# Gate logits with both halves of the gate weights side by side in one 40-column product

## The chip, the core and the metric

The kernel runs on one core of a Trainium2 chip. The engines named below are TensorE (PE; its weight loads are listed apart as PEld), VectorE (DVE), ScalarE (ACT), GpSimd (POOL) and SyncE (SP, which issues most DMAs). The metric is the device time of one execution in microseconds (us), the median of the runs. "The profile" is one execution taken by the hardware profiler.

## The reference, cut to what matters

Clustered attention over 4 batches of 8 heads with 768 positions of 64 numbers, and on its output a mixture of experts with two levels of gates: a group out of four, an expert out of four in that group.

```python
mask = q_assign[:, :, :, None] == k_assign[:, :, None, :]
scores = np.where(mask, scale * np.matmul(q, k.transpose(0, 1, 3, 2)), -1e9)
x = softmax(scores) @ v                      # (3072, 512) after the heads are joined
g_logits = x @ w_group                       # 4 columns
e_logits = xg @ w_expert[g]                  # 4 columns for each of 4 groups
h = np.maximum(xg[mask_e] @ w1[g, e], 0.0)   # 512 -> 1024
out[tok_idx] = combined[:, None] * (h @ w2[g, e])
```

The 4 + 16 gate columns stand in one weight matrix of 20 columns. Its product with x is what is called the logits here.

## The kernel before

**Precision.** Every large product is made of float16 halves: a number is held as a high part and a low part (the rest after rounding), and three products are summed in float32: high with high, high with low, low with high. The product of two low parts is left out.

**Stages.** The attention (function `attention`) goes through 32 heads with 9 units each. For a unit the code issues fine scores (`fine`, L342 and L343 on PE, the exponential L347 on ACT, the low part of the probabilities L349 on POOL), a coarse unit some way ahead (`coarse`, L302 on PE, a row maximum L305 on DVE), the product with V of a unit five units back (`av`, L368 and L369 on PE), and then one or two jobs out of a table of due times (`beside`): loads, splits, cluster assignments, and the gate's work. From about 421 us on the experts follow: a first expert with its rows of the first three batches (`part_a`, L950 and L968), and while it runs the gate's decision for the last batch, then the ranked experts (`ranks`).

**The gate.** Two heads fill 128 columns of x, so the logits of a batch are summed over four steps k, one after each second head. `Router.logits` does a step in two groups of three row tiles (i = 0, 1): six transposes (L592), one copy to SBUF (ACT, L595, tile xTr), nine products of 20 columns (PE, L600: three row tiles, three products each), and an addition to the running sum lg (DVE, a copy L604 at k = 0, an addition L606 later). There are 4 x 4 x 2 = 32 such groups. After k = 3 `Router.decide` takes the largest logit in every group of four and the softmax weights (DVE, L624 to L646, the exponential L635 on ACT), counts the rows of every expert with 12 products (PE, L651, L653, L655), works out the slot of every row (DVE, L658 to L663), and sends six scatters from POOL's queue to a table in DRAM (L674).

**What sets the order.** The sequence of the calls is written out by hand through due times; within a short horizon the framework's scheduler orders the instructions of an engine by a model of their times, so a changed duration can move its neighbours. Instructions of one engine run in that order, and an instruction that waits holds up all behind it on its engine.

**After the last decision.** When the last batch's rows have landed in the table, SP loads it to SBUF (tile tb, L1084), PE sorts it into slots (L1114), the gathers of the first ranked expert follow from it. On PE, 48 products of the first expert's second layer (L968) stand ahead of L1114, and 24 directly behind.

Of the kernel before, what the change touches and what calls it, by code (L numbers as in the profile page):

```python
# [11 lines left out]
F16 = mybir.dt.float16  # L12
BF16 = mybir.dt.bfloat16
F32 = mybir.dt.float32
I32 = mybir.dt.int32
AF = mybir.ActivationFunctionType
ALU = mybir.AluOpType
# [5 lines left out]
P = 128  # L23
# [4 lines left out]
WRS = 16.0  # L28
# [496 lines left out]
class Router:  # L525
# [9 lines left out]
    def setup(self):  # L535
        nc, const, N, E, BS, KD = self.nc, self.const, self.N, self.E, self.BS, self.KD
        wf = const.tile([P, KD, 20], F32, name="wf")
        nc.sync.dma_start(out=wf, in_=self.wr)
        self.WR = const.tile([P, 2, KD, 20], F16, name="WR")
        nc.vector.tensor_scalar(out=self.WR[:, 0], in0=wf, scalar1=WRS, scalar2=None, op0=ALU.mult)  # L540
        nc.vector.scalar_tensor_tensor(out=self.WR[:, 1], in0=wf, scalar=WRS, in1=self.WR[:, 0], op0=ALU.mult, op1=ALU.subtract)
        self.ones = const.tile([P, P], F16, name="ones")
        nc.vector.memset(self.ones, 1.0)
        self.low = const.tile([P, P], F16, name="low")
        nc.gpsimd.affine_select(out=self.low, in_=self.ones, pattern=[[1, P]], compare_op=ALU.is_gt, fill=0.0, base=0, channel_multiplier=-1)
        self.desc = const.tile([P, 30, 4], F16, name="desc4")
        nc.gpsimd.iota(self.desc, [[0, 30], [-1, 4]], base=4, channel_multiplier=0, allow_small_or_imprecise_dtypes=True)
        self.ebase = const.tile([P, E], F32, name="ebase")
        nc.gpsimd.iota(self.ebase, [[BS, E]], base=0, channel_multiplier=0, allow_small_or_imprecise_dtypes=True)
        self.cb = const.tile([P, E], F32, name="cb")  # L550
        NT = N // P
        self.pay = const.tile([P, NT, 2], F32, name="pay")
        nc.gpsimd.iota(self.pay[:, :, 0], [[P, NT]], base=0, channel_multiplier=1, allow_small_or_imprecise_dtypes=True)
        zrow = const.tile([P, 2 * KD], F16, name="zrow")
        nc.vector.memset(zrow, 0.0)
        nc.sync.dma_start(out=self.xbuf[N:N + 1].rearrange("o (p x) -> (o p) x", p=P), in_=zrow)
        em = self.em = const.tile([P, (E + 1) * BS // P // 5, 2], F32, name="em")
        nc.vector.memset(em[:, :, 0:1], float(N))
        nc.vector.memset(em[:, :, 1:2], 0.0)
        self.lg, self.last, self.sent, self.apart, self.done = {}, {}, [], True, -1  # L560

        self.reset()
# [8 lines left out]
    def store(self, b, xs):  # L571

        T = xs.shape[1]
        t0 = b * T
# [4 lines left out]
    def logits(self, b, xs, k, banks=None):  # L579

        nc = self.nc
        T = xs.shape[1]
        n = T // 2
        if k == 0:
            self.lg[b] = self.sm.tile([P, T, 20], F32, name="lg", bufs=2)
        for i in range(2):
            yield PSM, 0, 1
            pool, nm = (banks or [(self.psm, "psm")] * 2)[i]
# [5 lines left out]
            xT = self.sm.tile([P, n, 2, P], F16, name="xTr", bufs=2)  # L594
            self.last["a"] = nc.scalar.copy(out=xT, in_=tp)  # L595
            yield PSM, 1, 1
            lp = pool.tile([P, 512], F32, name=nm)[:, 0:n * 20].rearrange("p (c x) -> p c x", x=20)
            for c in range(n):
                for j, (a, w) in enumerate(((0, 0), (0, 1), (1, 0))):
                    nc.tensor.matmul(out=lp[:, c], lhsT=xT[:, c, a], rhs=self.WR[:, w, k], start=j == 0, stop=j == 2)  # L600
            yield
            lg = self.lg[b][:, n * i:n * i + n]
            if k == 0:
# [11 lines left out]

    def decide(self, b, early=None, then=None):
        nc, sm, E = self.nc, self.sm, self.E
        lg = self.lg[b]
        T = lg.shape[1]
        t0 = b * T  # L620
        G = T * 5
        lv = lg.rearrange("p t (g x) -> p (t g) x", x=4)
# [802 lines left out]
```

## Time and profile before

| | before |
|---|---|
| median of 3 runs | 783.28 us (782.55 to 783.51) |
| profiled execution: time | 782.34 us |
| profiled execution: span from first to last instruction | 780.6 us |
| mean granted TensorE clock | 0.978 of full speed |
| PE busy | 733.3 us (94%), 11086 products |
| PE weight loads busy | 626.5 us (80%) |
| DVE busy | 612.0 us (78%) |
| ACT busy | 466.8 us (60%) |
| POOL busy | 495.6 us (63%) |

The chain that ended last is of no use here: it holds the last four pieces alone, POOL's last scatter of 0.78 us among them. What limits a stretch is read from the busy times by stretch and from who waited for whom. PE runs its products pipelined: the duration of one (171 ns for 20 columns) is its way through the array, and what it costs the engine is the distance between two starts. In the timeline, equal instructions in a row are merged into one line with a count (x9), whose time runs from the first start to the last end; the distance between starts is then read from the start of the next line.

### The profile page before, as it was taken

What the parts mean: (1) busy time and instruction counts of PE and PEld (TensorE: products, weight loads), DVE (VectorE), ACT (ScalarE), POOL (GpSimd) and SP (SyncE); (2) the same over time, 40 slices, a digit from 0 to 9 for tenths busy, and PEclk for the clock granted to TensorE, in tenths of its full rate; (3) what the DMA queues carried; (4) which work ended last, traced back from release to release, by engine and by line L of the source; (5) the groups of instructions that cost most, each with busy time, mean ns of one, the idle gap of its engine ahead of it and who ended that gap; (6) DMA issues with size and microseconds to landing.
All of it is one profiled execution on the core that took longest, in us unless ns stands there. A gap on an engine that the chain in (4) does not pass through costs nothing. (4 is left out here: it accounts for less than half of the span.)

```text
span 780.6 us, 26678 instructions
## 1 busy us (share of the span) xinstructions
PE 733.3 (94%) x11086; PEld 626.5 (80%) x11086; DVE 612.0 (78%) x1209; ACT 466.8 (60%) x910; POOL 495.6 (63%) x497
## 2 busy tenths in 40 slices
PE   5899999999999999998999799999999999999991
PEld 3677888878888788886878677887789999999991
DVE  5998879899798988988875465867789888888830
ACT  5567877768777687775895255444344444555530
POOL 9578787778977788776972445434564655565330
PEclk7899999999999999999999999999999999999996
DMA  8856534435344352223312397866688688889600
GB/s 244 204 144 168 148 102 119 137 94 148 104 119 134 94 149 68 55 94 127 92 30 84 85 313 239 272 224 217 209 265 257 218 259 277 285 255 300 194 32 17
DMA packets 80392, 128.28 MB, mean 164 GB/s; under 512 B 8851, under 2 KB 47251, under 8 KB 80264
## 3 DMA queue, kind: packets, MB, share of 16 engines
q1 hardware_dynamic: 74492, 113.12, 48.9%
q0 software_dynamic: 5616, 13.35, 4.9%
q8 instruction: 88, 1.44, 0.8%
q14 instruction: 40, 0.33, 0.1%
q10 hardware_dynamic: 156, 0.03, 0.0%
HBM read 93.20 MB, written 14.11 MB: 137 GB/s over the span
## 5 line engine op out<-in xcount | busy, mean ns | idle before, releaser
L349 POOL TENSOR_TENSOR pl<-p 128x512 f16<-128x512 f32 x278 | 287.3, 1052 | 84.9 <-ACT p L347 80.7
L305 DVE TENSOR_REDUCE mpart<-psc 128x1 f32<-128x512 f32 (+1 forms) x282 | 189.8, 682 | 35.0 <-PE psc L302 32.8
L347 ACT ACTIVATE p<-psf 128x512 f32<-128x512 f32 x288 | 168.7, 595 | 56.1 <-PE psf L343 49.1
L368 PE MATMUL pso<-V,p 128*128 128x65 f16 x1152 | 161.6, 193 | 0.0
L368 PE MATMUL pso<-V,pl 128*128 128x65 f16 x1152 | 161.2, 194 | 0.0
L369 PE MATMUL pso<-V,pl 128*128 128x64 f16 x1152 | 161.0, 191 | 0.0
L369 PE MATMUL pso<-V,p 128*128 128x64 f16 x1152 | 160.8, 191 | 0.0
L342 PE MATMUL psf<-A 82*128 82x384 f16 (+2 forms) x576 | 143.7, 275 | 4.2 <-ACT p L347 2.8
L343 PE MATMUL psf<-B 128*128 128x384 f16 (+2 forms) x576 | 143.7, 274 | 0.0
L369 PEld LDWEIGHTS <-p 128*128 128x128 bf16 x1152 | 112.6, 98 | 21.4 <-issue 0.2
L368 PEld LDWEIGHTS <-p 128*128 128x128 bf16 x1152 | 112.2, 97 | 9.3 <-issue 1.4
L369 PEld LDWEIGHTS <-pl 128*128 128x128 f16 x1152 | 112.8, 98 | 0.7 <-issue 0.4
L302 PE MATMUL psc<-A 80*128 80x512 f16 (+1 forms) x376 | 108.4, 330 | 5.1 <-DVE mpart L305 3.3
L368 PEld LDWEIGHTS <-pl 128*128 128x128 f16 x1152 | 111.2, 97 | 0.3
L953 DVE SCALAR_TENSOR_TENSOR hl<-psh,hh 128x160 f16<-128x160 f32 (+14 forms) x136 | 49.9, 370 | 58.6 <-ACT hh L952 50.4
L952 ACT ACTIVATE hh<-psh 128x160 f16<-128x160 f32 (+14 forms) x136 | 46.6, 347 | 65.7 <-PE psh L950 64.3
L950 PE MATMUL psh<-xT,wh0a 128*128 128x288 f16 (+7 forms) x512 | 74.7, 255 | 0.0
L1011 POOL DMA_INDIRECT out_dram<-y,ri x32 | 38.5, 1203 | 55.1 <-ACT y L1010 48.8
L912 POOL DMA_INDIRECT xg<-xbuf,ri x32 | 43.5, 1359 | 39.8 <-PE psm L922 25.7
L343 PEld LDWEIGHTS <-B 128*128 128x128 f16 x576 | 56.6, 98 | 13.7 <-issue 5.3
L950 PE MATMUL psh<-xT,wh0b 128*128 128x272 f16 (+6 forms) x448 | 65.2, 254 | 0.9 <-ACT xT L924 0.5
L342 PEld LDWEIGHTS <-A 82*128 82x128 f16 x576 | 55.5, 98 | 12.0 <-DMA A<-mr 0.7
(308 smaller groups left out, 1776.9 us busy)
## 6 DMA issues: line engine op xcount, KB each, us to landing
st<-w SPq DMA_DIRECT2D x128, 512.0 KB
B<-parts SPq DMA_DIRECT2D x64, 192.0 KB
kx<-kT SPq DMA_DIRECT2D x16, 384.0 KB
qx<-qT SPq DMA_DIRECT2D x16, 384.0 KB
vx<-vr SPq DMA_DIRECT2D x16, 384.0 KB
A<-parts SPq DMA_DIRECT2D x32, 192.0 KB
xbuf<-xs SPq DMA_DIRECT2D x4, 1536.0 KB
A<-mk SPq DMA_DIRECT2D x56, 24.0 KB
```

Source lines behind the costliest of these rows:

```text
L302: last["mm"] = nc.tensor.matmul(out=pc[:, off:off + k1 - k0], lhsT=QA[h % 8][0:80, c * P:(c + 1) * P], rhs=KA[h % 8][0:80, k0:k1], start=T ...
L305: nc.vector.tensor_reduce(out=(mp[:, 0, 0:1], mp[:, :, 1], mp[:, 1, 0:1])[i], in_=pc.rearrange("p (a x) -> p a x", a=n), axis=AX.X, op=ALU ...
L342: nc.tensor.matmul(out=o, lhsT=KA[h % 8][0:82, ks], rhs=QA[h % 8][0:82, q0:q1], start=True, stop=False)
L343: nc.tensor.matmul(out=o, lhsT=KBs[h][:, ks], rhs=QBs[h][:, q0:q1], start=False, stop=True)
L347: cfg["exp"] = nc.scalar.activation(out=p32, in_=pf, func=AF.Exp, scale=QK / (SQ * SQ))
L349: lo = (nc.vector if u in (EARLY if h < 2 else DVE_LO[h % 8] if h < NH - 2 else DVE_END) else nc.gpsimd).tensor_tensor(out=pl, in0=p32, in ...
L368: nc.tensor.matmul(out=O[:, col:col + 65], lhsT=p[:, bs], rhs=vh, start=c == 0 and q == 0 and i == 0, stop=False, skip_group_check=True)
L369: nc.tensor.matmul(out=O[:, col:col + 64], lhsT=p[:, bs], rhs=vl, start=False, stop=c == NCH - 1 and i == 1, skip_group_check=True)
L912: self.got = nc.gpsimd.indirect_dma_start(out=xg[0:n].rearrange("p a d -> p (a d)"), out_offset=None, in_offset=bass.IndirectOffsetOnAxis( ...
L950: self.mm = nc.tensor.matmul(out=ph[:, 0:M], lhsT=w[:, k, fs], rhs=xT[:, a, k], start=i == 0, stop=i == 3 * KD - 1)
L952: nc.scalar.activation(out=hh[:, f], in_=ph[:, 0:M], func=AF.Relu)
L953: self.ev = nc.vector.scalar_tensor_tensor(out=hl[:, f], in0=ph[:, 0:M], scalar=0.0, in1=hh[:, f], op0=ALU.max, op1=ALU.subtract)
```

## The change

The gate weights WR are stored as [row, k, part, column] instead of [row, part, k, column], so the 20 columns of the high part and the 20 of the low part lie side by side. For a row tile two products of 40 columns (high and low part of x against both parts of the weights) take the place of three products of 20, so the product of the two low parts is now in it as well. The running sum lg holds 40 columns for a row tile, and `decide` begins with an addition of the two halves into a new tile lgs.

```diff
-        self.WR = const.tile([P, 2, KD, 20], F16, name="WR")
+        self.WR = const.tile([P, KD, 2, 20], F16, name="WR")
...
-            self.lg[b] = self.sm.tile([P, T, 20], F32, name="lg", bufs=2)
+            self.lg[b] = self.sm.tile([P, T, 2, 20], F32, name="lg", bufs=2)
...
-            lp = pool.tile([P, 512], F32, name=nm)[:, 0:n * 20].rearrange("p (c x) -> p c x", x=20)
+            lp = pool.tile([P, 512], F32, name=nm)[:, 0:n * 40].rearrange("p (c w x) -> p c w x", w=2, x=20)
             for c in range(n):
-                for j, (a, w) in enumerate(((0, 0), (0, 1), (1, 0))):
-                    nc.tensor.matmul(out=lp[:, c], lhsT=xT[:, c, a], rhs=self.WR[:, w, k], start=j == 0, stop=j == 2)
+                for a in range(2):
+                    nc.tensor.matmul(out=lp[:, c].rearrange("p w x -> p (w x)"), lhsT=xT[:, c, a], rhs=self.WR[:, k].rearrange("p w x -> p (w x)"), start=a == 0, stop=a == 1)
...
-        lg = self.lg[b]
-        T = lg.shape[1]
+        both = self.lg[b]
+        T = both.shape[1]
+        lg = sm.tile([P, T, 20], F32, name="lgs")
+        nc.vector.tensor_tensor(out=lg, in0=both[:, :, 0], in1=both[:, :, 1], op=ALU.add)
```

Lines behind the addition (L621) are two higher in the changed file: L624 of before is L626 there.

The scheduler places the decision's instructions differently. DVE at the decision of the first batch, before; mpart is the coarse scores' row maximum, rmx to roe are the decision's tiles:

```order
L606 TENSOR_TENSOR lg<-psm,lg 128x60
L624 TENSOR_REDUCE rmx<-lg 128x30
L626 TENSOR_TENSOR req<-lg,rmx 128x120
L305 TENSOR_REDUCE mpart_198<-psc 128x2
L627 TENSOR_TENSOR req<-req,desc_499 128x120
L634 TENSOR_TENSOR rdf<-lg,rmx 128x120
L629 TENSOR_REDUCE rmw<-req 128x30
L631 TENSOR_TENSOR roh<-req,rmw 128x120
L305 TENSOR_REDUCE mpart_198<-psc 128x1
L637 TENSOR_REDUCE rse<-rdf 128x30
L639 TENSOR_TENSOR roe<-roh 128x96
```

DVE at the same place in the changed kernel:

```order
L606 TENSOR_TENSOR lg<-psm,lg 128x120
L621 TENSOR_TENSOR lgs<-lg 128x120
L626 TENSOR_REDUCE rmx<-lgs 128x30
L305 TENSOR_REDUCE mpart_198<-psc 128x2
L628 TENSOR_TENSOR req<-lgs,rmx 128x120
L636 TENSOR_TENSOR rdf<-lgs,rmx 128x120
L629 TENSOR_TENSOR req<-req,desc_499 128x120
L305 TENSOR_REDUCE mpart_198<-psc 128x1
L631 TENSOR_REDUCE rmw<-req 128x30
L639 TENSOR_REDUCE rse<-rdf 128x30
L633 TENSOR_TENSOR roh<-req,rmw 128x120
L641 TENSOR_TENSOR roe<-roh 128x96
```

The addition L621 has come in, and both row maxima still stand between the last logits and roe, each one or two places earlier in the decision. The decisions of the second and third batch read alike.

DVE in the second half of the last batch's decision, before; hl (L953) are evictions of the first expert's hidden layer:

```order
L643 TENSOR_REDUCE res<-rss 128x6
L644 TENSOR_SCALAR res<-res 128x6
L953 SCALAR_TENSOR_TENSOR hl<-psh,hh 128x288
L645 SCALAR_TENSOR_TENSOR res<-rse,res 128x6
L658 TENSOR_TENSOR rps<-psm,cb 128x96
L646 RECIPROCAL pay<-res 128x6
L659 TENSOR_TENSOR rps<-rps,roe 128x96
L664 TENSOR_TENSOR cb<-psm,cb 128x16
L661 TENSOR_REDUCE rds<-rps 128x6
```

DVE at the same place in the changed kernel:

```order
L645 TENSOR_REDUCE res<-rss 128x6
L955 SCALAR_TENSOR_TENSOR hl<-psh,hh 128x288
L646 TENSOR_SCALAR res<-res 128x6
L660 TENSOR_TENSOR rps<-psm,cb 128x96
L647 SCALAR_TENSOR_TENSOR res<-rse,res 128x6
L955 SCALAR_TENSOR_TENSOR hl<-psh,hh 128x288
L648 RECIPROCAL pay<-res 128x6
L661 TENSOR_TENSOR rps<-rps,roe 128x96
L666 TENSOR_TENSOR cb<-psm,cb 128x16
L663 TENSOR_REDUCE rds<-rps 128x6
```

A second eviction of the hidden layer now stands between the counts and the slots. On PE, the products of the first expert are reordered with it: before, 12 of L968 stood between the sixth and the seventh of the eight chunks of L950; now the seventh chunk follows the sixth directly and 7 of L968 stand ahead of the eighth. The 48 products of L968 ahead of L1114 are the same in number.

## Rows read from the trace of the kernel before

**Rows 1.** Busy by stretch: length, PE, PEld, DVE, ACT, POOL busy (instructions), PEclk, DMA share, GB/s

```profile
120.00:150.00 30.00, 29.85 (x586) 24.93 (x584) 26.09 (x59) 23.94 (x46) 22.35 (x22) 1.00 0.44 134
360.00:390.00 30.00, 27.57 (x501) 22.42 (x500) 23.79 (x46) 22.77 (x44) 26.10 (x26) 1.00 0.45 139
```

**Rows 2.** Waits of PE, whole span: us in total, times, longest us

```profile
PE psm L651 <- DVE roe L639: 3.8, 3, 1.3
```

**Rows 3.** Groups by line: count | busy us, mean ns | idle before

```profile
L600 PE MATMUL psm<-WR,xTr 128*128 128x20 f16 x279 | 11.6, 171 | 0.0
L606 DVE TENSOR_TENSOR lg<-psm,lg 128x60 f32<-128x60 f32 x23 | 4.9, 215 | 1.6 <-PE psm L600 1.5
```

**Rows 4.** Timeline of PE, first logits: start us, us, instruction

```profile
94.18 0.19 PE L369 MATMUL pso<-V,pl 128*128 128x64 f16 x1
94.21 0.37 PE L600 MATMUL psm<-WR,xTr 128*128 128x20 f16 x9
94.44 0.22 PE L342 MATMUL psf<-A 82*128 82x128 f16 x1
```

**Rows 5.** Timeline of PE, counts of the last decision; L653 has 80 to 16 columns

```profile
428.80 0.28 PE L653 MATMUL psm<-roe,ones 128*128 128x80 f16 x5
428.94 0.29 PE L655 MATMUL psm<-roe,ones 128*128 128x16 f16 x6
429.09 0.28 PE L950 MATMUL psh<-xTA,wh 128*128 128x288 f16 x1
```

**Rows 6.** Timeline of DVE, decision of the first batch

```profile
153.34 0.22 DVE L606 TENSOR_TENSOR lg<-psm,lg 128x60 f32<-128x60 f32 x1
153.59 0.28 DVE L624 TENSOR_REDUCE rmx<-lg 128x30 f32<-128x120 f32 x1
153.91 0.85 DVE L626 TENSOR_TENSOR req<-lg,rmx 128x120 f16<-128x120 f32 x1
154.68 0.68 DVE L305 TENSOR_REDUCE mpart<-psc 128x2 f32<-128x512 f32 x1
155.28 0.45 DVE L627 TENSOR_TENSOR req<-req,desc 128x120 f16<-128x120 f16 x1
...
156.15 0.82 DVE L631 TENSOR_TENSOR roh<-req,rmw 128x120 f16<-128x120 f16 x1
...
157.67 0.57 DVE L639 TENSOR_TENSOR roe<-roh 128x96 f16<-128x96 f16 x1
```

**Rows 7.** Timeline of POOL, same stretch

```profile
152.58 4.25 POOL L349 TENSOR_TENSOR pl<-p 128x512 f16<-128x512 f32 x4 [1.02 <-ACT p L347]
157.09 1.04 POOL L349 TENSOR_TENSOR pl<-p 128x512 f16<-128x512 f32 x1 [0.26 <-ACT p L347]
```

**Rows 8.** Timeline of PE, same stretch

```profile
158.29 0.20 PE L651 MATMUL psm<-roe,low 128*128 128x96 f16 x1 [1.27 <-DVE roe L639]
```

**Rows 9.** One line's instructions in all four decisions: min/median/max ns

```profile
L626 DVE TENSOR_TENSOR req<-lg,rmx x4: 284/849/849, 153.9 to 427.1; 128x120 f16<-128x120 f32 x4
```

**Rows 10.** Timeline of DVE, decision of the last batch

```profile
429.13 0.45 DVE L953 SCALAR_TENSOR_TENSOR hl<-psh,hh 128x288 f16<-128x288 f32 x1
429.50 0.15 DVE L645 SCALAR_TENSOR_TENSOR res<-rse,res 128x6 f32<-128x6 f32 x1
```

**Rows 11.** Timeline of PE, first expert up to the slots

```profile
438.51 0.41 PE L968 MATMUL psy<-hh,wh 128*128 128x288 f16 x2 [0.99 <-ACT hh L952]
440.01 0.28 PE L968 MATMUL psy<-hh,wh 128*128 128x288 f16 x1 [1.09 <-ACT hh L952]
...
445.98 1.58 PE L1114 MATMUL psm<-perm,tb 16*128 16x16 f32 x12 [1.65 <-DMA tb<-table]
447.50 1.15 PE L968 MATMUL psy<-hh,wh 128*128 128x288 f16 x8
448.49 2.00 PE L968 MATMUL psy<-hh,wl 128*128 128x288 f16 x8
```

**Rows 12.** Busy by stretch, one of the rows at half clock

```profile
450.00:451.00 1.00, 1.00 (x6) 0.60 (x4) 0.56 (x1) 0.00 (x0) 0.69 (x2) 0.50 1.03 395
```

More of the change, by code (lines that the diff above doesn't have):

```diff
@@ L538, in setup @@
         nc.sync.dma_start(out=wf, in_=self.wr)
-        self.WR = const.tile([P, 2, KD, 20], F16, name="WR")
-        nc.vector.tensor_scalar(out=self.WR[:, 0], in0=wf, scalar1=WRS, scalar2=None, op0=ALU.mult)
-        nc.vector.scalar_tensor_tensor(out=self.WR[:, 1], in0=wf, scalar=WRS, in1=self.WR[:, 0], op0=ALU.mult, op1=ALU.subtract)
+        self.WR = const.tile([P, KD, 2, 20], F16, name="WR")
+        nc.vector.tensor_scalar(out=self.WR[:, :, 0], in0=wf, scalar1=WRS, scalar2=None, op0=ALU.mult)
+        nc.vector.scalar_tensor_tensor(out=self.WR[:, :, 1], in0=wf, scalar=WRS, in1=self.WR[:, :, 0], op0=ALU.mult, op1=ALU.subtract)
         self.ones = const.tile([P, P], F16, name="ones")
```

## The prediction

> **What bounds the kernel now.** I read the busy times by stretch first. From 90 us, where the gate's first logits are, to 421 us the attention runs at PE's pace: PE is busy 29.85 of 30 us in a plain stretch, while DVE, the next engine, has 26.1 [rows 1]. So a product less on PE is worth its distance between starts. PE's list of waits then shows the one thing of the gate that holds it: L651, the first count of a decision, waits for the tile roe of DVE, three times and 3.8 us in all [rows 2], 1.27 of it at the first [rows 8]. PE stands behind that product, so a longer decision on DVE is paid in full. Later in that part PE has other idle time too (27.57 of 30 [rows 1]). After 421 us a different chain rules: last logits, decision, scatters, the table's load, and the slots L1114, for which PE waits 1.65 us [rows 11]. Behind L1114 PE is busy again to the end, so what moves L1114 moves the end.
>
> **The products.** Nine products of 20 columns take 0.23 us from the first start to the next instruction, 25.6 ns each [rows 4]. A group has six now. No row shows 40 columns. From below, six products of 16 columns take 0.15 us, 25 ns each; five of 80 to 16 columns, 48 on the mean, take 0.14 us, 28 ns each [rows 5]; 64 columns take 30 ns [rows 4]. So 40 columns cost 25 to 30 ns. I take 26, since the nearest row above, 48 on the mean, has two products of 64 and 80 in it, which pull it up. A group then takes 0.156 us and saves 0.074 (bounds 0.05 and 0.08). Of the 32 groups, 24 lie in the first three batches and 6 of the last batch ahead of the end of the attention: 24 x 0.074 = 1.78 and 6 x 0.074 = 0.44, in sum **-2.2 us** (bounds -1.5 and -2.4). The last two groups lie in the chain to L1114 and are counted there. [...]
>
> **The wider additions.** L606 and L604 go from 60 to 120 elements. L606 has 215 ns [rows 3]; a DVE instruction over 120 elements with nothing in its way has 284 [rows 9]. That is 0.07 more, 32 times, 2.2 us on DVE. It lies beside PE's work, with 4 to 6 us of DVE free in 30 [rows 1]; if that cover were gone it would cost up to the 2.2. Only the last of each batch heads a chain that PE waits for. The strided writes of WR happen once in the setup and I cost them at nothing, beside the attention's first loads.
>
> **The decisions of the first three batches.** L621 is a new link between the last logits and roe, where PE stands. Its size is that of L626, which reads lg from SBUF too: 0.28 us alone and 0.85 in these three decisions [rows 9]. The difference is POOL: L626 begins at 153.91 in the middle of a POOL subtraction and ends at 154.76; four of them run back to back from 152.58 to 156.83, 1.06 us each, so the second ends about 154.7 [rows 6, 7]. L627, L631 and L639 end about 0.1 us behind a POOL instruction in the same way, while the reduction L624 keeps its 0.28. [...]
>
> I walk the new order against these POOL times. L606 now ends at 153.62 and L621 starts at 153.65, just inside the second POOL subtraction, and ends where L626 ended, at 154.76. The reduction L624 takes it to 155.06, the row maximum (0.68) to 155.66. The comparison L626 ends at about 155.8, as L627 did at 155.73. The next two with two SBUF inputs meet the fourth subtraction and end about 157.0. Row maximum and two reductions take it to 158.1 (0.68, 0.28, 0.28, each starting a little before the last ends). L631 then waits out the fifth subtraction, which ends at 158.13, and ends at 158.37; L639 alone takes 0.28 and ends at 158.66. Before, it ended at 158.24. So the chain grows by **0.42 us**, though L621 alone seems to cost 0.85 or 1.1, because other waits for POOL fall away. The low bound is -0.5: of the waits in the rows (L626 0.57, L627 0.17, L631 0.54, L639 0.29 over 0.28) a luckier phase could drop two, about 0.9, against 0.39 for the new link alone (0.07 + 0.32, the step from L624 to L626). The high bound is +1.1, the 0.07 and one POOL subtraction of 1.04 more. Three times: **+1.3 us** (bounds -1.5 and +3.3). Behind L651 wait all of PE's products, and the exponentials that need them.
>
> **The last decision.** POOL is quiet there, so L621 costs its 0.32, the wide L606 0.07, the shorter group of products gives 0.07 back. The order puts a second eviction L953 between the counts and the slots, one step of 0.37 (429.13 to 429.50 [rows 10]). So the scatters start 0.32 + 0.07 - 0.07 + 0.37 = **0.69 us** later (bounds 0.3, if that eviction finds a gap, and 0.75), and table, load and L1114 with them. PE's earlier seventh chunk gains nothing, because PE waits 1.65 us at L1114 anyway [rows 11]; it only gathers PE's idle time there. On SP the register loads for the experts' numbers come a little later among the weight loads, on ACT a few exponentials pass a copy; PE is full there, so I give them nothing.
>
> **Sum.** -2.2 + 1.3 + 0.69 = -0.2 us. The profiled execution took 782.34 us, so the changed one should take 782.1. The median of the runs lies 0.94 above the profiled execution, so **783.0 us** is the forecast. About 0.2% (1.6 us) is what a measurement of this kernel can tell from no change: below 781.7 counts as faster, above 784.9 as slower. The forecast's own range, by a few tenths on each of the three decisions, is 782.0 to 784.5.
>
> **Rivals.** (1) *The products' gain comes through.* If the phase against POOL turns lucky, the three decisions grow by nothing, and the second eviction finds a gap: -2.2 + 0 + 0.3 = -1.9, giving 781.4; with each product at 25 ns 781.2. For it: before, 1.6 us of a decision of 4.9 us are waits for POOL, so there is something to lose. Against it: all three decisions have the same phase, and the walk shows three waits. (2) *The new addition collides with POOL, slower.* If L621 waits for a whole subtraction and no later wait falls away, a decision grows by 1.1: -2.2 + 3.3 + 0.69 = +1.8, giving 785.1. It decides from a growth of 0.5 a decision on ((2.2 - 0.69) / 3), only a tenth above my value; to be seen as slower it takes 1.0. [...] (4) *Wide products cost twice the narrow ones.* At 51 ns a group takes 0.31, and 30 groups lose 2.4 us where the sum has a gain of 2.2: 787.6. The 30 ns of 64 columns speak against it.
>
> **Chances and range.** Forecast 0.57, rival 1 0.19, rival 2 0.12, rival 3 0.10, rival 4 0.02. Faster by over 0.2%: most of rival 1 and a little of the forecast, 0.19. Slower: most of rival 2, half of rival 3, rival 4 and a little of the forecast, 0.20. Within: 0.61. The range goes from rival 1 to rival 2, 781.1 to 785.2, which leaves out about 2 in 10.
>
> **What would show it.** In the profile after: 192 products L600 in groups of six that take about 0.156 us from the first start to the next instruction; L606 at about 0.28; L621 near 0.3 at the last decision and around 1 us at the others; PE's wait at L651 near 1.7 us each instead of 1.27; distance from one decision to the next shorter by 8 x 0.074 - 0.42, about 0.2 us; L1114 at about 445.8; PE's wait ahead of it longer than 1.65. It is wrong if PE's wait at L651 stays at 1.3 or goes over 2.2, if a group of six takes more than 0.18, or if the stretch at 0.50 after L1114 is much longer or gone.

## The result and the profile of the kernel after

The kernel after takes **793.64 us** (median of four runs, 791.12 to 796.41) where the kernel before took 782.91 in the runs beside it: the ratio is put at 1.0124 with a 95% interval of 1.0095 to 1.0153. It is slower, by 10.7 us between the medians; 783.0 was forecast, with a range to 785.2. The profiled execution took 796.41 us with a span of 794.6, the longest of the four; before it was 782.34 and 780.6, so the two profiles lie 14.0 us apart. The mean granted clock was 0.959 in that execution of the kernel after, and 0.978, as in the profile of before, in the one of 791.12, so the clock is not the whole loss. L641, L653, L778 and L1116 of the kernel after are L639, L651, L776 and L1114 of before.

The products did what they should. Group of lines L600 and L606 (count, busy us, mean ns, idle before; [rows 3] answer), and the start of a group of six on PE's timeline:

```profile
L600 PE MATMUL psm<-WR,xTr 128*128 128x40 f16 x186 | 9.6, 181 | 0.0
L606 DVE TENSOR_TENSOR lg<-psm,lg 128x120 f32<-128x120 f32 x23 | 6.4, 279 | 2.0 <-PE psm L600 2.0
```

```profile
152.91 0.31 PE L600 MATMUL psm<-WR,xTr 128*128 128x40 f16 x6
153.06 0.27 PE L342 MATMUL psf<-A 82*128 82x256 f16 x1
```

Six products of 40 columns take 0.15 us from the first start to the next instruction where nine of 20 took 0.23 [rows 4], and the wide addition 0.28 where the narrow one took 0.21 [rows 3].

The loss is in PE's waits (whole span: us in total, times, longest us; [rows 2] answers the first) and in the stretches around them (length, busy us of each engine, granted clock, DMA share, GB/s; [rows 1] answer the first two):

```profile
PE psm L653 <- DVE roe L641: 7.1, 4, 2.3
PE psf L342 <- ACT p L347: 6.2, 5, 4.5
PE psm L1116 <- DMA tb<-table: 5.1, 1, 5.1
...
PE psm L592 <- DVE lg L606: 1.9, 1, 1.9
```

```profile
120.00:150.00 30.00, 29.58 (x577) 24.65 (x575) 26.12 (x59) 23.92 (x46) 22.18 (x22) 1.00 0.44 134
360.00:390.00 30.00, 24.56 (x391) 19.31 (x388) 20.26 (x45) 17.76 (x34) 20.41 (x20) 0.89 0.36 107
160.00:162.00 2.00, 2.00 (x24) 1.69 (x23) 1.62 (x6) 1.01 (x3) 0.53 (x1) 0.50 0.01 4
260.00:262.00 2.00, 2.00 (x23) 1.56 (x22) 1.59 (x7) 1.79 (x3) 1.04 (x1) 0.50 0.05 8
```

The wait for the decision is 2.3 us instead of 1.3, PE runs at half clock (a granted clock of 0.50) behind the first two decisions, where it had 1.00 behind all three in the profile of before, and the longest wait for the exponentials L347 has grown from 1.3 to 4.5 us.

Decision of the first batch on DVE ([rows 6] answer), two POOL subtractions inside it ([rows 7] answer), PE behind it ([rows 8] answers), and last the exponential of the decision on ACT, in the kernel before and in the kernel after:

```profile
153.25 0.28 DVE L606 TENSOR_TENSOR lg<-psm,lg 128x120 f32<-128x120 f32 x1
153.57 1.17 DVE L621 TENSOR_TENSOR lgs<-lg 128x120 f32<-128x120 f32 x1
154.77 0.28 DVE L626 TENSOR_REDUCE rmx<-lgs 128x30 f32<-128x120 f32 x1
...
155.57 0.27 DVE L628 TENSOR_TENSOR req<-lgs,rmx 128x120 f16<-128x120 f32 x1
155.76 1.12 DVE L636 TENSOR_TENSOR rdf<-lgs,rmx 128x120 f32<-128x120 f32 x1
...
157.90 0.27 DVE L633 TENSOR_TENSOR roh<-req,rmw 128x120 f16<-128x120 f16 x1
158.20 0.98 DVE L641 TENSOR_TENSOR roe<-roh 128x96 f16<-128x96 f16 x1
```

```profile
153.56 1.04 POOL L349 TENSOR_TENSOR pl<-p 128x512 f16<-128x512 f32 x1
...
157.92 1.14 POOL L349 TENSOR_TENSOR pl<-p 128x512 f16<-128x512 f32 x1 [1.19 <-ACT p L347]
```

```profile
159.23 0.24 PE L653 MATMUL psm<-roe,low 128*128 128x96 f16 x1 [2.30 <-DVE roe L641]
```

```profile
155.96 0.30 ACT L635 ACTIVATE rdf<-rdf 128x120 f32<-128x120 f32 x1 [0.35 <-DVE rdf L634]
```

```profile
156.91 0.30 ACT L637 ACTIVATE rdf<-rdf 128x120 f32<-128x120 f32 x1 [1.39 <-DVE rdf L636]
```

L621, L636 and L641 each begin behind the start of a POOL subtraction (L621 by 0.01 us) and end a little over 0.1 us behind its end. The one that L641 meets is the fifth, and it has moved: it began at 157.09 before [rows 7] and begins at 157.92 now. The comparison L636 came late itself, ACT waited 1.39 us for it instead of 0.35, and behind that exponential in ACT's queue stood the exponential L347 which the fifth subtraction reads. All three decisions of the kernel after have this wait on ACT (1.39, 1.40 and 1.39 us).

To place the loss I compare the starts of the 288 exponentials L347, in order of time: the lag is the start of one in a kernel less the start of the same one in the kernel before. Single ones scatter, so a value is the median of those about that time. Each row is one profiled execution. Last column: the end of the span.

| time in the kernel before | 150 | 249 | 346 | 362 | 374 | 418 | end |
|---|---|---|---|---|---|---|---|
| lag of the kernel after, us | 0.0 | +2.1 | +5.2 | +5.8 | +10.4 | +12.9 | +14.0 |

The decisions begin at 153, 250 and 347 us. So 5.8 us have come by the end of the three decisions, with the saving of the products already taken off, 7.1 from the stretch between 362 and 418 us, and 1.1 from all behind it.

In that second stretch the first expert is begun: DVE works out its number, SP loads its weights with that number as address, ACT converts them (L778), with exponentials queued behind. ACT, SP's issues, POOL's queue and the DMA in the kernel after:

```profile
373.57 1.06 ACT L778 ACTIVATE wh<-st 128x1024 f16<-128x1024 f32 x1 [4.63 <-DMA st<-w]
```

```profile
367.70 2.25 SPq L758 DMA_DIRECT2D st<-w  x4
```

```profile
366.36 0.98 POOL L676 DMA_INDIRECT table<-pay,rdi  x1 [0.15 <-DVE ft L805]
```

```profile
368.00:370.00 2.00, 1.94 (x38) 1.40 (x34) 1.56 (x3) 0.94 (x2) 1.45 (x2) 1.00 0.50 14
370.00:372.00 2.00, 1.23 (x21) 0.89 (x21) 0.06 (x1) 0.00 (x0) 0.57 (x1) 1.00 0.62 113
372.00:374.00 2.00, 0.00 (x0) 0.00 (x0) 0.00 (x0) 0.43 (x1) 0.00 (x0) 1.00 1.04 379
```

and the same places in the kernel before:

```profile
364.65 1.06 ACT L776 ACTIVATE wh<-st 128x1024 f16<-128x1024 f32 x1 [1.50 <-DMA st<-w]
```

```profile
360.84 2.13 SPq L756 DMA_DIRECT2D st<-w  x4
```

```profile
361.05 0.98 POOL L674 DMA_INDIRECT table<-pay,rdi  x1 [0.16 <-DVE ft L808]
```

```profile
362.00:364.00 2.00, 1.93 (x40) 1.53 (x37) 1.56 (x3) 1.15 (x3) 1.28 (x3) 1.00 0.92 308
```

Before, POOL sent the third decision's first scatter 0.21 us behind SP's first weight load (by their starts in the two queues), and the loads moved 308 GB/s within about a microsecond. After, it was sent 1.34 us ahead, and the loads moved 14 and 113 GB/s for four microseconds before they were fast. ACT stood 4.63 us instead of 1.50. The second wait of this stretch is DVE's for the first expert's table (tile idA), with an addition of the logits behind it for which PE's L592 waits 1.9 us (DVE's waits for the table, before and after: us in total, times, longest):

```profile
DVE idA L838 <- DMA tabA<-table: 1.1, 2, 0.7
```

```profile
DVE idA L840 <- DMA tabA<-table: 2.9, 2, 2.0
```

### The profile page after: what moved, and what is told of

Read it like the earlier page. It is cut to its first block, busy times and chain, and to the rows that moved or that the text cites. A ratio compares the mean times of both kernels' runs of the same rounds, so it can differ in the third digit from the quotient of the medians.

```text
span 794.6 us, 26490 instructions
## 1 busy us (share of the span) xinstructions
PE 741.4 (93%) x10990; PEld 631.5 (79%) x10990; DVE 610.1 (77%) x1213; ACT 466.9 (59%) x910; POOL 493.7 (62%) x497
## 5 line engine op out<-in xcount | busy, mean ns | idle before, releaser
L347 ACT ACTIVATE p<-psf 128x512 f32<-128x512 f32 x288 | 169.5, 595 | 64.9 <-PE psf L343 61.3
L368 PE MATMUL pso<-V,p 128*128 128x65 f16 x1152 | 164.5, 195 | 0.0
L368 PE MATMUL pso<-V,pl 128*128 128x65 f16 x1152 | 163.8, 195 | 0.0
L369 PE MATMUL pso<-V,pl 128*128 128x64 f16 x1152 | 163.7, 193 | 0.0
L369 PE MATMUL pso<-V,p 128*128 128x64 f16 x1152 | 163.6, 193 | 0.0
L342 PE MATMUL psf<-A 82*128 82x384 f16 (+2 forms) x576 | 147.0, 280 | 6.4 <-ACT p L347 6.2
L343 PE MATMUL psf<-B 128*128 128x384 f16 (+2 forms) x576 | 146.9, 280 | 0.0
L369 PEld LDWEIGHTS <-p 128*128 128x128 bf16 x1152 | 113.8, 99 | 22.3 <-issue 1.6
L368 PEld LDWEIGHTS <-p 128*128 128x128 bf16 x1152 | 113.3, 98 | 9.0 <-issue 1.1
L302 PE MATMUL psc<-A 80*128 80x512 f16 (+1 forms) x376 | 111.2, 338 | 2.9 <-DVE mpart L305 1.7
```

The costliest lines, as they stand in the source:

```text
L302: last["mm"] = nc.tensor.matmul(out=pc[:, off:off + k1 - k0], lhsT=QA[h % 8][0:80, c * P:(c + 1) * P], rhs=KA[h % 8][0:80, k0:k1], start=T ...
L342: nc.tensor.matmul(out=o, lhsT=KA[h % 8][0:82, ks], rhs=QA[h % 8][0:82, q0:q1], start=True, stop=False)
L343: nc.tensor.matmul(out=o, lhsT=KBs[h][:, ks], rhs=QBs[h][:, q0:q1], start=False, stop=True)
L347: cfg["exp"] = nc.scalar.activation(out=p32, in_=pf, func=AF.Exp, scale=QK / (SQ * SQ))
L368: nc.tensor.matmul(out=O[:, col:col + 65], lhsT=p[:, bs], rhs=vh, start=c == 0 and q == 0 and i == 0, stop=False, skip_group_check=True)
L369: nc.tensor.matmul(out=O[:, col:col + 64], lhsT=p[:, bs], rhs=vl, start=False, stop=c == NCH - 1 and i == 1, skip_group_check=True)
```

## The experiments

All ratios are against the kernel before on the same chip, with 95% intervals. In the expected texts GpSimd is POOL, ScalarE ACT, VectorE DVE, TensorE PE.

**First: is it the addition or the products?** Run e1 makes the products wide and keeps the rest of the kernel before; the sum takes the first 20 columns alone, so x's product with the low part of the weights is left out.

```diff
-                for j, (a, w) in enumerate(((0, 0), (0, 1), (1, 0))):
-                    nc.tensor.matmul(out=lp[:, c], lhsT=xT[:, c, a], rhs=self.WR[:, w, k], start=j == 0, stop=j == 2)
+                for a in range(2):
+                    nc.tensor.matmul(out=lp[:, c].rearrange("p w x -> p (w x)"), lhsT=xT[:, c, a], rhs=self.WR[:, k].rearrange("p w x -> p (w x)"), start=a == 0, stop=a == 1)
...
+                nc.vector.tensor_tensor(out=lg, in0=lp[:, :, 0], in1=lg, op=ALU.add)
```

> The 40-column products alone: the running sum keeps 20 columns and takes the first half of each product, and the decision has no addition. Left out is x times the low part of the weights. Theory 1 (the added link in the decision costs the time, the products gain): 780 to 782 us, PE's wait at the counts stays at about 1.3 us three times, mean clock 0.978. Theory 2 (the wide products, or the order they bring, cost the time): 790 us or more.

Measured: 793.29 us, 1.0096 [1.0068, 1.0123], slower, with no addition at the head of the decision. The lag is -0.4 us at 150, +4.9 at 346, +7.7 at 418. DVE's instructions stand in the order of before, yet the same instruction is four times as long (one line's instructions in all four decisions, min/median/max ns; the kernel before, then e1; then its start on DVE beside POOL's in the first decision, before and e1):

```profile
L634 DVE TENSOR_TENSOR rdf<-lg,rmx x4: 271/272/277, 155.7 to 427.3; 128x120 f32<-128x120 f32 x4
```

```profile
L634 DVE TENSOR_TENSOR rdf<-lg,rmx x4: 276/1140/1140, 155.2 to 434.8; 128x120 f32<-128x120 f32 x4
```

```profile
155.65 0.27 DVE L634 TENSOR_TENSOR rdf<-lg,rmx 128x120 f32<-128x120 f32 x1
```

```profile
155.69 1.14 POOL L349 TENSOR_TENSOR pl<-p 128x512 f16<-128x512 f32 x1
```

```profile
155.25 1.14 DVE L634 TENSOR_TENSOR rdf<-lg,rmx 128x120 f32<-128x120 f32 x1
```

```profile
155.21 1.03 POOL L349 TENSOR_TENSOR pl<-p 128x512 f16<-128x512 f32 x1
```

Before, DVE began 0.04 us ahead of POOL and was through in 0.27, with POOL's subtraction at 1.14 instead of 1.04; in e1 it began 0.04 us behind and took 1.14. A shift of less than a tenth of a microsecond, the size of the products' own saving, puts DVE on the wrong side. As in the kernel after, ACT then waits for this comparison (1.29 us), POOL's fifth subtraction comes late, and the product roe takes 0.99 us behind it. So the loss comes without the addition.

Runs e2, e3 and e4 vary the addition. e2: the narrow products of before, and an addition of a zero tile in the decision. e3: the kernel after with a reduction in place of the addition, which reads one operand. e4: wide products, both halves added from PSUM to a sum of 20 columns, no addition in the decision.

```diff
+        nc.vector.tensor_tensor(out=lg, in0=both, in1=self.zero, op=ALU.add)
...
-        nc.vector.tensor_tensor(out=lg, in0=both[:, :, 0], in1=both[:, :, 1], op=ALU.add)
+        nc.vector.tensor_reduce(out=lg, in_=both.rearrange("p t w x -> p t x w"), axis=AX.X, op=ALU.add)
...
+                nc.vector.tensor_tensor(out=lg, in0=lp[:, :, 0], in1=lg, op=ALU.add)
+            nc.vector.tensor_tensor(out=lg, in0=lp[:, :, 1], in1=lg, op=ALU.add)
```

> The kernel before with three products of 20 columns, and at the head of the decision one addition of a zero tile of the same size, both inputs in SBUF. Theory 1: the time is as of the changed kernel plus the 2.2 us that its products save, 792 to 798 us, PE's wait at the counts 2.2 us or more, and the granted clock at half behind some decisions. Theory 2: 783 to 784 us.

> The changed kernel with the two halves summed by a reduction over both, one SBUF input in place of two. Theory 1 (the link is dear because it waits for POOL's subtraction): it takes about 0.4 us instead of 1.17, the decision grows by 0.3 to 0.8, the time is 782 to 787 us. Theory 3 (any link more at this place costs as much, whatever it waits for): 791 to 796 us as the changed kernel.

> 40-column products, and both halves added to a 20-column running sum by two additions of 60 elements per group, straight from PSUM; no addition at the decision's head. The chain to the counts has one more short link that does not wait for POOL. Theory 1: growth of 0.25 to 0.5 us at a decision, 781 to 784 us. Theory 3: 791 to 796 us.

Measured: e2 1.0135 [1.0104, 1.0166], e3 1.0155 [1.0131, 1.0178], e4 1.0071 [1.0051, 1.0092]. Only e2 came as the theory of the added link had it; e3 and e4 were to lie at 781 to 787 us and took 797.38 and 791.57. In each, some two-operand instructions of the decision wait for POOL, though not the same ones (in the first decision L623 and L638 take 1.17 and 1.12 us in e2, L635 and L628 1.12 and 1.05 in e4). In e3 the reduction itself takes 0.41 us and no longer 1.17, and the wait moves to two instructions behind it (DVE, first decision):

```profile
154.34 0.41 DVE L621 TENSOR_REDUCE lgs<-lg 128x120 f32<-128x240 f32 x1
...
155.60 0.90 DVE L628 TENSOR_TENSOR req<-lgs,rmx 128x120 f16<-128x120 f32 x1
156.43 1.11 DVE L636 TENSOR_TENSOR rdf<-lgs,rmx 128x120 f32<-128x120 f32 x1
```

The wide products without the addition cost time (e1), and an addition without the wide products does too (e2), so neither is the cause by itself. What follows is theory P: an edit that moves the decision against POOL's subtractions can cost a subtraction or two; the kernel before stood well by 0.04 us.

**Second: take away the collision, or PE's clock.** e5 is the kernel after with 36 products nobody reads ahead of the wait at the counts. e6 is the kernel before with the decision's tiles in PSUM. e7 is e4 with the same tiles in PSUM.

```diff
+        if not early:
+            for _ in range(36):
+                nc.tensor.matmul(out=rk[:, 256:384], lhsT=self.low, rhs=self.ones, start=True, stop=True, skip_group_check=True)
...
-        mx = sm.tile([P, G], F32, name="rmx")
+        sc = self.psm.tile([P, 512], F32, name="psm")
+        mx = sc[:, 0:G]
...
-        eq = sm.tile([P, G, 4], F16, name="req")
+        eq = sc[:, G:5 * G].rearrange("p (g x) -> p g x", x=4)
...
-        nc.vector.tensor_tensor(out=oe, in0=oh[:, :, 1:5], in1=oh[:, :, 0].broadcast_to([P, T, 4, 4]), op=ALU.mult)
+        nc.vector.tensor_tensor(out=oe, in0=o4, in1=o0.broadcast_to([P, T, 4, 4]), op=ALU.mult)
```

> The kernel after, and in the decisions of the first three batches 36 products of 128 columns into a part of the counts' bank that nobody reads, behind the products on the other parts and ahead of the wait for the one-hots' product (L641 of the kernel after). They keep TensorE at work for about 2 us of a wait of 2.3 us and delay nobody if the wait lasts. Theory P (the collision with GpSimd sets the wait, and the halved clock behind it is a further cost of its own): the waits on DVE stay as in the kernel after (L621 and L636 about 1.1 us), the two half-clock stretches behind the decisions (159 and 258 us) are gone, and with them the growth of the lag of 1.7 us and 3.4 us there; 788 to 792 us instead of 793.6. Rival C (the clock falls for another reason than the wait at the decision): the same half-clock stretches, 793 to 797 us.

> The kernel before with its three products of 20 columns, and the maxima, the equality mask and four fifths of the one-hots of the decision in a PSUM bank instead of SBUF, so that none of the operations on the path to the one-hots' product reads two operands from SBUF; one operation more (the one-hots in two parts). Theory P (two-operand operations in SBUF wait for a whole subtraction of GpSimd when they begin behind it): no operation of that path takes over 0.45 us while GpSimd runs, the wait at the counts falls from 1.3 us to under 0.5, no half clock behind a decision, 778 to 782 us. Rival L (what counts is the length of DVE's chain, with or without GpSimd): PSUM operands and one operation more make the chain longer by 0.3 to 0.6 us, and the time is 785 us or more.

> The wide products of the kernel after, the two sums added as in the run with two additions from PSUM, and the decision's tiles in PSUM as in the run beside it. Theory P: the saving of the products, 2 us, shows at last, since nothing on the path to the one-hots' product waits for GpSimd: 775 to 781 us, no half clock behind the three decisions. Rival R (the wide products or their order in the queues cost the time by themselves): 788 to 793 us, as in the other runs with wide products, whatever the decision does.

Measured: e5 796.10 us, 1.014 [1.0117, 1.0162]; e6 793.06, 1.0091 [1.0067, 1.0114]; e7 793.12, 1.0085 [1.0051, 1.0118]. The times missed what theory P had forecast in all three and lie where the rivals had them, or just above; the lags tell why.

| lag, us | 150 | 249 | 346 | 362 | 374 | 418 |
|---|---|---|---|---|---|---|
| e5, filler | -0.8 | +2.0 | +5.0 | +6.0 | +5.9 | +8.7 |
| e6, narrow, in PSUM | -0.1 | +0.5 | +0.8 | -0.5 | +2.8 | +3.1 |
| e7, wide, in PSUM | +1.5 | +1.7 | +0.9 | -0.5 | +4.4 | +8.2 |

In e6 and e7 the lag does not grow over the three decisions (150 to 362 us): no wait at the counts is left in PE's list, and the product that had taken up to 0.98 us takes 0.25 in all four decisions (e7):

```profile
L644 DVE TENSOR_TENSOR roe<-psm,ro x4: 250/251/251, 158.8 to 437.0; 128x96 f16<-128x96 f32 x4
```

So theory P holds for the decisions, and the rest of the loss has another place. e5 settles nothing: PE kept its clock behind the decisions (1.00 from 159 to 162 us, behind the first), but with the filler in the program the planner put two of ACT's conversions ahead of an exponential, so its lag is not the clock's alone. The clock's price is seen better in three kernels that are the same up to 350 us (after, and e8 and e14 below). Their PE waited 2.3 us at each decision. Where half clock followed one of the first two, the lag had grown by 1.9, 3.6 and 2.9 us some 30 us later, where it did not, by 2.5, 1.5 and 1.7. The means lie 0.9 us apart, but the two groups overlap, so about 1 us for the clock is an estimate from six decisions. At 362 us these three executions of the same work had lags of 5.8, 5.3 and 4.0 us.

**Third: the scatter ahead of the weight loads.** e8 is the kernel after with the scatters of the third decision later in POOL's queue, e10 is e7 and e11 is e6 with the same; e9 is the kernel before with its first scatter earlier.

```diff
-            for _ in range(1 if early else 4 if then else 5):
+            for _ in range(1 if early else (7, 4, 4, 3, 3, 3)[c] if then else 5):
...
-            for _ in range(1 if early else 4 if then else 5):
+            for _ in range(1 if early else (1, 7, 4, 4, 4, 4)[c] if then else 5):
```

> The kernel after, with the six scatters of the third decision's rows later in GpSimd's queue: the first stands behind three more of its subtractions, the last where it was. In the kernel after, that first scatter runs 1 us ahead of the first expert's weight loads, and the loads move 14 to 113 GB/s for 4 us before they reach 300 and more; in the kernel before it runs 3 us behind their start, and they move 308 GB/s at once. Theory S (the scatter ahead of the loads makes them start slowly): the loads move 300 GB/s within 1 us of their first packet, ACT's wait for them falls from 4.6 us to 2.5 or less, the half clock at 374 us goes, the lag grows from 362 to 418 us by 3.5 us or less instead of 7; 789 to 791.5 us. Rival D (the loads come late only because their address does, and start slowly for another reason): the wait stays over 4 us, 793 to 796 us.

> The kernel before, with the first scatter of the third decision's rows three subtractions earlier in GpSimd's queue, so that it runs ahead of the first expert's weight loads; nothing else is changed. Theory S: the loads start slowly as in the kernel after, ACT's wait for them grows from 1.5 us to 3.5 to 5, PE stands for 3 us or more and then runs at half clock; 1.005 to 1.01 times the kernel before. Rival D: the loads start at once, and the time is that of the kernel before within 0.3%.

> The wide products with the decision's tiles in PSUM, as in the run of that name, and the third decision's scatters moved behind the weight loads as in the first run here. That kernel was level with the kernel before up to 362 us (a lag of -0.8) and lost 5.5 us at 374 and 3 at 399. Theory S: those are gone or halved, and the time is 784 to 789 us. Rival D: 791 to 795 us as without the move.

> The kernel before with its narrow products, the decision's tiles in PSUM, and the third decision's scatters moved behind the weight loads. Without the move its lag was -0.5 us at 362 and +3.2 at 374. Theory S: the lag at 374 is 1 us or less, and the time falls from 1.009 of the kernel before to 1.003 to 1.006, since the 6 us that it loses behind 428 us have another cause. Rival D: 1.009 again.

Measured: e8 1.0155 [1.0109, 1.0201], e9 0.9991 [0.9968, 1.0014], e10 1.0073 [1.0044, 1.0102], e11 1.0105 [1.0069, 1.0141]. By the times theory S fell: e8 (798.51 us) and e10 (793.94) came slower than it allows, e11 did not improve on e6, and e9 stayed level with the kernel before. By the rows it is half right. In e8 the loads move 190 and 370 GB/s where they moved 14 and 113, and ACT waits 2.7 us instead of 4.6:

```profile
368.00:370.00 2.00, 2.00 (x27) 1.35 (x27) 1.08 (x2) 0.41 (x1) 2.00 (x2) 1.00 0.78 190
370.00:372.00 2.00, 0.69 (x17) 0.56 (x16) 0.00 (x0) 0.86 (x1) 0.04 (x1) 1.00 1.00 370
```

```profile
ACT wh L778 <- DMA st<-w: 2.7, 1, 2.7
```

From 362 to 374 us the lag grows by 1.8 us instead of 4.6 (in e11 by 0.8 where e6 had 3.3). But then DVE's longest wait for the table is 3.5 us, and at 418 e8 is 12.4 us behind, as the kernel after was (12.9). In e9 the scatter was sent 4.5 us ahead of the loads; they moved 247 GB/s, and ACT waited 1.7 us. In e10 the loads started fast (246 GB/s from 361 to 363 us) and ACT still waited 4.2: it came there early, with a lag of about -3 us at 362. Among all 18 profiles the loads start slowly in the seven where the scatter comes 1.3 to 2.0 us ahead of them, and in none of the other eleven; e8, e10 and e11 are three of those eleven, made so by the scatters' place alone. What a slow start costs is decided by the queues: ACT reaches the conversion before the weights can be there, and DVE the table.

**Fourth: the two waits at the head of a queue.** e14 is the kernel after, e12 is e7 and e13 the kernel before, all with the conversions three exponentials later in ACT's queue and the table's reading two turns later in DVE's. e15 is e6 with the same (so e12 with narrow products), and e16 is e12 once more, beside e15.

```diff
-        for q in range(4 + 2):
+        for q in range(4 + 4):
...
-            if q >= 2:
-                yield from self.split_beside(chunks[q - 2], *self.WA, 0, q - 2)
+            if q >= 4:
+                yield from self.split_beside(chunks[q - 4], *self.WA, 0, q - 4)
...
-        for _ in range(FIRST + 1):
+        for _ in range(FIRST + 3):
```

> The kernel after, with the conversions of the first expert's weights three exponentials later in ScalarE's queue and the reading of its table two turns later in VectorE's. Theory Q (the loss from 361 to 418 us is two waits at the head of a queue): ScalarE's wait for the weights falls from 4.6 us to 1.5 or less, the wait for the table from 2.0 to under 0.5, the half clock at 374 and 408 us goes, and the lag grows by 2 us or less from 361 to 418 instead of 7.1; 787 to 790 us. Rival K (the chain from the decision to weights and table sets the time): the waits move elsewhere, the lag grows by 5 us or more, 792 to 797 us.

> The wide products with the decision's tiles in PSUM, and the same later places in the two queues. Without them that kernel stood 0.5 us ahead of the kernel before at 361 us and 8.2 behind at 418. Theory Q: at 418 us it is at most 2 us behind, and the time 782 to 787 us (0.995 to 1.002 of the kernel before). Rival K: 5 us behind or more, 790 to 795 us.

> The kernel before, with the same later places in the two queues. Its wait for the weights is 1.5 us and for the table 0.7. Theory Q: PE's gaps of 1.5 us at 367 and 0.8 us at 396 go, a gain of 1 to 2 us by 418, of which the end may keep nothing; 0.995 to 1.002. Rival K: the first expert, which then has less time, is late at 421 us and the last decision with it: 1.003 or more.

> The kernel before with its three products of 20 columns, the decision's tiles in PSUM, and the conversions and the table's reading in the later places of their queues: the run wide_psum_slack without the wide products. Theory W (the wide products save 0.07 us a group, and nothing hides it here): at 346 us the wide kernel is 1.5 to 2 us ahead of this one, and of that 0.5 to 2 us are left at the end; this kernel 784 to 787 us where that one has 783 to 785. Rival N (the saving is taken back at the next wait): no difference within 0.2%.

> The run wide_psum_slack again, the same kernel, beside the narrow one. Theory W: 0.995 to 0.999 of the kernel before, and 0.5 to 2 us below the narrow one. Rival N: 0.997 to 1.001, and level with the narrow one.

Measured: e14 789.96 us, **1.0064** [1.0038, 1.0091], where the kernel after had 1.0124; e12 782.86, **0.9968** [0.9941, 0.9995]; e13 784.43, 0.9989 [0.9973, 1.0005]; e15 790.86, 1.0056 [1.0026, 1.0087]; e16 788.23, 1.0009 [0.9978, 1.0040]. e14, e12 and e13 came as theory Q had them; e15 and e16 came slower than theory W had them.

| lag, us | 150 | 249 | 346 | 362 | 374 | 418 |
|---|---|---|---|---|---|---|
| e14, after + slack | +0.1 | +1.7 | +2.8 | +4.0 | +2.0 | +2.5 |
| e12, wide, in PSUM, slack | -0.4 | -2.3 | -3.8 | -5.5 | -4.0 | -3.6 |
| e16, e12 once more | +0.6 | +0.3 | -0.4 | -2.0 | -1.3 | -0.5 |
| e15, narrow, in PSUM, slack | -0.4 | -0.3 | 0.0 | -1.3 | -1.9 | -1.6 |
| e13, before + slack | +2.2 | +2.0 | +2.0 | +2.0 | 0.0 | +0.2 |

The rows of e12 and e16, one kernel, lie up to 3.4 us apart, and e13 stands at +2.2 at 150 us, where it is still the kernel before. So I read growth within a row, and differences that come back in several pairs.

e14 against the kernel after shows the second half of the loss: from 362 to 418 us the lag falls by 1.5 us where it grew by 7.1, and the wait for the weights is gone (ACT's timeline of e14; no wait stands behind the row):

```profile
371.01 1.06 ACT L778 ACTIVATE wh<-st 128x1024 f16<-128x1024 f32 x1
```

In e14 alone the place in the queues is not separated from the loads, which came 0.16 us behind the scatter there and started fast (190 GB/s from 366 to 368 us). The other pairs separate them. With fast loads and the old places e8 still lost 7.1 us between 362 and 418. With slow loads in both (scatter 1.8 to 2.0 us ahead) e7 lost 8.7 us, and e12 and e16, the same with the later places, 1.9 and 1.5; e6 lost 3.6 and e15 gained 0.3. So the two places decide, whether the loads start slowly or not. Which of the two does more is not shown, since every run moves both; in e14 DVE still waited 1.2 us for the table, where under 0.5 was expected.

e12 has neither loss. It is below the kernel before in its first run and level with it in its second (e16), so it is not shown to beat it; what is shown is that the same wide products come with a loss of 1.2% in one arrangement, and with none that can be told from zero in another (decision in PSUM, later places).

The products' own saving shows between 150 and 346 us, where 16 groups lie, for which the measured 0.23 and 0.15 us a group give 1.2 us. There the lag grows by 0.9, 0.8 and 0.4 us in the narrow kernels with the decision in PSUM (e6, e11, e15) and falls by 0.6, 1.1 and 1.0 in the wide ones (e7, e10, e16; by 3.4 in e12): 1.5, 2.0 and 1.4 us apart. At the end of the kernel it is not shown. The medians of e15 and e16, on one chip, lie 2.6 us apart, but their intervals overlap a little, and in the profiles e16 is behind e15 at 418 us, so that difference came behind it.

Not all of what e12 gained up to 418 us is there at the end. PE comes to L1114 earlier and waits longer for the same table (PE's timeline of e12, where L1114 is L1119; 1.65 us before [rows 11]):

```profile
444.10 0.60 PE L1119 MATMUL psm<-perm,tb 16*128 16x16 f32 x2 [5.55 <-DMA tb<-table]
```

The part behind 418 us added between 1.1 us (after) and 8 to 10 us (e6, e15) to the lag, 5.9 in e14; in e9 and e13, whose times are level with the kernel before, it added 4.0 and about 5. The one profiled execution of the kernel before is among its quickest, so I read no cause out of that part; it stays open, and with it why e15 is slower than the kernel before at a lag of -1.6 at 418 us.

## Why the prediction was wrong

**The products, right.** Six in 0.15 us and L606 at 0.28 came as written, and the three pairs of narrow and wide kernels show the saving between 150 and 346 us. In the kernel after two places ahead of the end took more than the 2.2 us.

**The decisions, the first step that failed.** The walk gave a growth of 0.42 us for a decision; PE's wait grew from 1.27 to 2.30 us, 1.03 each. Up to the last two instructions the walk came out: L621 ended at 154.74 (forecast 154.76), the comparison at 155.84 (155.8), the next two with two SBUF inputs at 157.01 (157.0), the reductions at 157.98 (158.1). What failed is the step in which "L631 then waits out the fifth subtraction, which ends at 158.13" and L639 "alone takes 0.28". It left POOL's fifth subtraction where it stood in the kernel before. But the walk's own delay of the comparison rdf, to 156.88 instead of 155.92, held ACT's queue, and the subtraction came 0.83 us later. The first of the two (L633 now) began 0.02 us ahead of it and took 0.27; the second (L641) met it and ended at 159.18 where 158.66 was forecast. The same wait on ACT stands in e1, e2 and e3 (1.29 to 1.32 us). That this order of events makes the loss is read from the rows; the experiments show that it needs the waits for POOL, since it goes with them in e6 and e7.

The high bound of +1.1 and rival 2 had the size of this growth, but by another way, "no later wait falls away". Three later waits did fall away (L628, L629 and L633 take 0.21 to 0.27 us now), one came (L636) and one grew (L641), so the agreement in size is luck. And a forecast near 0.42 with "a few tenths" of range was finer than the rows allow, where 0.08 us in the start of an instruction makes 0.27 or 1.14 us of it (before and e1).

**Behind a decision, missed.** The forecast paid a longer wait in full but with nothing behind it. Three decisions of 1.03 make 3.1 us, and the 16 groups of products between 150 and 346 us should have given 1.2 back; the lag at 362 us is 5.8. About 1 us each behind the first two is PE at half clock, by the estimate from the kernels that are the same up to there. The rest, about 1 us and those 1.2, I did not separate.

**The first expert's weights and table, the second step that failed.** The prediction gave the register loads and the order on ACT nothing, because "PE is full there". No term and no rival named ACT's wait for the weights, though it stood in the trace of before with 1.50 us and exponentials behind it. 7.1 us came there, more than from the decisions. The step at fault is that a delay at a decision was taken to end at PE. The decision of the third batch also feeds the address of a load; a late address and a scatter that now runs ahead of the loads (0.21 us behind in the kernel before, 1.34 ahead after) put a wait of 4.6 us at the head of ACT's queue and one of 2.0 at the head of DVE's. e14, e12, e16 and e15 take that loss out by the later places in the two queues.

**The last decision, right.** L621 takes 0.28 us there, with POOL idle for 9.8 us ahead of the first scatter; from the last L606 to the first scatter it is 4.9 us, 4.4 before, a growth of 0.5 where 0.69 was forecast for the scatters in all. PE's wait ahead of L1116 went to 5.1 us, as "longer than 1.65" had it.

**The rivals.** Rival 1 is excluded by the time; rival 4 by the 0.15 us of a group. Rival 2 named the collision of L621 and the size of a decision's growth, but ended at 785.1, because it too stopped at the decision. Rival 3, with its chance of 0.10, was a longer stretch of PE's half clock behind L1114. No run shows what sets its length, and what it would cost was an estimate; the stretch at 0.50 there [rows 12] did grow, from 3.4 to 6.8 us, but the part behind 418 us adds as much or more to the lag without the change (e9, e13), so its price is not separated. Of the prediction's own signs of being wrong, a wait over 2.2 us at the counts came, with 2.30.

## What to carry to other kernels

Where DVE instructions with two SBUF operands run beside POOL, do not walk a new order through them to a tenth: give each either its own time or that of POOL's instruction on top (0.27 or 1.14 us here), or keep one operand in PSUM, which took the wait away here (0.25 us in e7). Do not hold POOL's times fixed in such a walk either: its input may stand in a queue that waits for the chain you are walking, as ACT's did here for 1.39 us. Then follow a delay beyond the engine that waits: list every load whose address or data hangs on the late result, and what stands behind the instruction that consumes it in its queue (a wait of 4.6 us at the head of ACT's here). A step whose data come to such a queue just in time should be given a later place, so that a small shift ahead of it does not stop the queue: with the later places the lag from 362 to 418 us fell by 1.5 us (e14) where it had grown by 7.1.

## What the runs showed of the hardware

- The same DVE instruction, with the same neighbours, takes 0.27 us when it begins 0.04 us ahead of a POOL subtraction (which then takes 1.14 us instead of 1.04) and 1.14 us when it begins 0.04 us behind (before and e1). With one operand in PSUM the product roe took 0.25 us in all four decisions (e7) where it had taken up to 0.98.
- PE's clock did not fall to 0.50 behind waits at the counts of 1.3 us (0 of 9 decisions of the kernel before, e9 and e13). It did behind those of 1.7 us in e4 and 2.1 us in e1 (3 of 3 each), behind those of 1.8 us in 1 of 3 of e3 and of 2.2 us in 2 of 3 of e2, and behind those of 2.3 us in 2 of 3 of the kernel after and 1 of 3 of e8 and of e14, so one length of wait can end either way.
- Weight loads that follow an indirect scatter by 1.3 to 2.0 us (after, e3, e6, e7, e12, e15, e16) moved 14 to 144 GB/s, by stretches of 2 us, in their first 4 us; with the scatter behind them (before, e8), 0.16 us ahead (e14) or 4.5 us ahead (e9) they moved 190 to 308 in the 2 us that begin about a microsecond behind their start. What slows them I did not find out.
